# Linear attention and a snake-activated feed-forward layer on one core: the kv product in quarters of the tensor array

## The chip, the core and the metric

The kernel runs on one core of a Trainium2 chip. A core has five engines with queues of their own: TensorE (PE in the profile; its weight loads are listed apart as PEld), VectorE (DVE), ScalarE (ACT), GpSimd (POOL) and SyncE (SP). They wait for each other through semaphores. Matrix products read on-chip memory with 128 partitions and write to accumulators of eight banks per partition. The metric is the device time of one launch, in microseconds; the median of three runs of the kernel before is 287.68 us (287.46 to 288.37).

## The reference

The first half is a linear attention over 8 batches, 8 heads, 576 rows and 64 dimensions; the second a feed-forward layer with a snake activation over the 4608 rows.

```python
q_s = softmax(q, over the 64 dimensions)
k_s = softmax(k, over the 576 rows)
kv  = einsum('bhsd,bhse->bhde', k_s, v)          # 64 x 64 for each batch and head
x   = einsum('bhsd,bhde->bhse', q_s, kv)         # then heads side by side: 4608 x 512
h   = x @ w_in                                   # 4608 x 2048
g   = h + sin(alpha * h) ** 2 / alpha
out = g @ w_out                                  # 4608 x 512
```

## The kernel before

Rows. A batch has 576 rows, laid out as 64 partitions by J = 9 rows each. Eight heads are stored as four pairs `i` and two row halves `e`: partitions 0 to 63 hold heads of even number, partitions 64 to 127 those of odd number. So 128 partitions hold both, and a tile `st_q`, `st_k` or `st_v` is 128 x 4 x 9 x 64.

Attention of a batch. ACT takes the exponential of k into `ke` (bf16, line 118). v is cast into `vb`, where each head has 65 columns: 64 of v and one of ones, so that the product also gives the sum of the exponentials (lines 134 to 137, 299). `kv_mm(b, ii)` (line 163) handles two of the four `i`, that is two heads of each row half, in one go: for each of the nine j and each of the two row halves e, one product with 64 contracted rows, 128 weight columns (two heads of `ke`) and 130 moving columns (the same two heads of `vb`), summed over j in `kvp`, a tile of two accumulator banks, one for each e. Only the two diagonal blocks of 64 x 65 of each 128 x 130 result are used; the others mix two heads. `kv_norm` (line 176) takes the reciprocals of the sums (DVE, line 181), and two multiplies (line 184) put the diagonal blocks, divided by the sums, into `kbd`, a block-diagonal matrix whose other blocks were set to zero once. `attn_out` or `attn_chunk` (lines 220, 228) then multiplies `kbd` with the transposed, normalized exponentials of q (`qT`), two heads at a time, and copies the result to `xT`.

Feed-forward. For each of nine groups of 512 rows, `mm_h` (line 248) makes sixteen h blocks with four 512-column products each; ACT takes the sine, ACT, POOL or DVE the square; `combine` (line 264, DVE) writes `g`; `mm_o` (line 268) sums sixteen products into each of four outputs of the group, and `evac_o` copies and stores them.

Order. The order on each engine is the order in the program (a manual schedule). Batches 0 and 1 run at the start, where `kv_mm(b, 0)` and `kv_mm(b, 1)` are separate bursts of 18 products, each with its own `kvp` and `kv_norm` (lines 344 and 358, 451 and 454). The start of the feed-forward waits for batch 0. For batches 2 to 7 the two calls follow each other, 36 products in one burst, and one `kv_norm` (lines 516 to 518, and `attn_back`, lines 540 to 542). From batch 3 on the burst lies between the h and output products of the feed-forward groups, and its result is first used by `attn_out` several blocks later. PE gets a weight load (PEld) and a product from each call of `nc.tensor.matmul`, so a burst of 36 products is 72 instructions.

Of the kernel before, what the change touches and what calls it, by code (L numbers as in the profile page):

```python
# [15 lines left out]
F32 = mybir.dt.float32  # L16
BF16 = mybir.dt.bfloat16
AX = mybir.ActivationFunctionType
ALU = mybir.AluOpType
# [4 lines left out]
def kernel(  # L24
# [14 lines left out]
    nc = tc.nc  # L39
    ctx.enter_context(nc.allow_non_contiguous_dma(reason="layout"))  # L40
    B, H, S, D = q.shape
# [3 lines left out]
    J = 9  # L45
# [12 lines left out]
    small = ctx.enter_context(tc.tile_pool(name="small", bufs=2))  # L58
# [55 lines left out]
    A = {}  # L114
# [48 lines left out]
    def kv_mm(b, ii, pool, split=False):  # L163

        if ii == 0 or split:
            A["kvp", b] = pool.tile([128, 2, 512], F32, name="kvp", tag="a")
        kvp, ke, vt = A["kvp", b], A["ke", b], vb[b % 2]
        for j in range(J):
            for e in range(2):
                r = slice(64 * e, 64 * e + 64)  # L170
                nc.tensor.matmul(kvp[:, e, ii * 130:(ii + 1) * 130],  # L171
                                 ke[r, j, ii * 128:(ii + 1) * 128],
                                 vt[r, j, ii * 130:(ii + 1) * 130],
                                 start=(j == 0), stop=(j == J - 1))

    def kv_norm(b, i0=0, i1=2):

        kt, m = kbd[b % 2], i1 - i0
        kvr = small.tile([128, 2, 2, 2], F32, name="kvr")[:, :, 0:m]
        src = A["kvp", b][:, :, i0 * 130:i1 * 130].rearrange("p e (ii x c) -> p e ii x c", ii=m, x=2)  # L180
        nc.vector.reciprocal(kvr, src[:, :, :, :, D])
        for x in range(2):
            r = slice(64 * x, 64 * x + 64)
            nc.vector.tensor_tensor(kt[r, :, i0:i1, r], src[r, :, :, x, 0:D],  # L184
                                    kvr[r, :, :, x].unsqueeze(3).to_broadcast([64, 2, m, D]), op=ALU.mult)

    def q_tile(b):
        if ("qT", b) not in A:
# [153 lines left out]
    exp_half("k", 0, 1)  # L342
    warm_up(2)
    kv_mm(0, 0, ps_e, split=True)
    warm_up(3)
    kv_norm(0, 0, 1)
    tp1 = ps_e.tile([128, 8, 128], BF16, name="tp", tag="a")
    q_transpose_ii(0, 1, 0, 8, tp1)
# [7 lines left out]
    ACT_CP(A["qT", 0][:, 1, 0:8], tp1)  # L356
    ACT_CP(xT[:, 1, 0:MF], xp[1])
    kv_mm(0, 1, ps_e, split=True)
    kv_norm(0, 1, 2)
    xp = [ps_e.tile([128, 2, MF], F32, name="xp", tag="a")[:, 0] for _ in range(2)]  # L360
    for e in range(2):
# [35 lines left out]
    with ES:  # L397
# [51 lines left out]
        exp_to(A["qe", 1][:, 7:J], q78)  # L449
        take(os, 3)  # L450
        kv_mm(1, 0, ps_e, split=True)
        kv_norm(1, 0, 1)
        take(os, 3)
        kv_mm(1, 1, ps_e, split=True)
# [102 lines left out]
    for t in range(3, nT):  # L557
        b = t + 1 if t + 1 < B else None
# [60 lines left out]
```

## Time and profile before

| | |
|---|---|
| median of three runs | 287.68 us (287.46 to 288.37) |
| span of the profiled execution, first to last instruction | 285.8 us |
| median less span | 1.9 us |
| PE busy | 272.6 us, 95% |
| kv products, line 171 | 288, 9.9 us busy (union), 216 ns each |
| kv weight loads, line 171 | 288, 8.4 us busy, 93 ns each |
| h products, line 248 | 512 of them as `hp`, 129.0 us |
| output products, line 268 | 479 of them as `op`, 121.9 us |
| reciprocals, line 181 | 6 of 128x8 at 198 ns, 4 of 128x4 at 180 ns |
| multiplies into `kbd`, line 184 | 12 of 64x256 at 422 ns, 8 of 64x128 at 289 ns |

The page gives a span for the profiled execution and no other time of its own; its span is set beside the median of the runs. Busy time of a group is the union of its instructions, so overlapping ones count once; the mean is the recorded duration of one, which for a product includes its way through the pipeline (a 512-column product is recorded with 379 ns, while its successor starts 216 ns after it). "Idle before" is the time in which the engine did nothing before such an instruction. A few per cent of the product records are missing.

### The profile page before, as it was taken

How to read it: one execution, taken by the hardware profiler on the slowest of the kernel's cores; microseconds unless marked ns; L12 is line 12 of the kernel's file. 1: busy time of each engine (PE TensorE's matmuls, PEld its weight loads, DVE VectorE, ACT ScalarE, POOL GpSimd, SP SyncE). 2: the span in 40 equal slices, each digit the busy share in tenths (PEclk: the TensorE clock that was granted, in tenths of full speed). 3: DMA queues.
4: the chain of work that ended last, by engine and by line, in shares of the span. 5: the costliest groups of instructions: out<-in, count | busy, mean ns of one | idle time of the engine just before them, and what ended most of it. 6: DMA issues, size and time to landing. Idle time of an engine off the chain costs nothing.

```text
span 285.8 us, 4247 instructions
## 1 busy us (share of the span) xinstructions
PE 272.6 (95%) x1541; PEld 130.8 (46%) x1569; DVE 192.6 (67%) x291; ACT 226.0 (79%) x321; POOL 80.6 (28%) x75
## 2 busy tenths in 40 slices
PE   2899999999999999999999999999999999999994
PEld 1444454445454454444544454445444444444443
DVE  4857967999999658766785677667674555555321
ACT  4898748999489999899889988998877777777400
POOL 2869512773477480005300530041000000000000
PEclk9999999999999999999999999999999999999999
DMA  7999999843999984139711990016011111111242
GB/s 261 308 204 243 260 397 407 312 169 78 275 222 412 372 169 105 37 69 406 218 38 39 359 292 20 22 36 155 1 39 37 37 37 39 37 38 41 46 100 73
DMA packets 38581, 45.77 MB, mean 160 GB/s; under 512 B 16528, under 2 KB 22432, under 8 KB 38560
## 3 DMA queue, kind: packets, MB, share of 16 engines
q1 hardware_dynamic: 33376, 40.57, 46.3%
q0 software_dynamic: 4992, 4.79, 9.7%
q8 instruction: 12, 0.20, 0.3%
q10 hardware_dynamic: 192, 0.14, 0.2%
q14 instruction: 9, 0.07, 0.1%
HBM read 36.71 MB, written 9.44 MB: 161 GB/s over the span
## 4 chain that ended last, share of the span: by engine, by line
PE 74%; DVE 9%; DMA 7%; ACT 4%; issue 3%; POOL 2%; SPq 0%; ACTq 0%
PE op L268 33%; PE hp L248 33%; DMA st_v<-in_v_dram 5%; ACT s L254 3%; DVE g L264 2%; POOL s L258 2%; PE kvp L171 2%; DVE qs L150 2%; PE xp L220 2%; DMA st_q<-in_q_dram 1%; PE op L589 1%; PE hh L248 1%; DVE vb L137 1%; DVE qn L152 1%; DVE kbd L184 1%
## 5 line engine op out<-in xcount | busy, mean ns | idle before, releaser
L264 DVE SCALAR_TENSOR_TENSOR g<-s,inva_sb,hp 128x512 bf16<-128x512 f32 x130 | 96.0, 745 | 58.4 <-ACT s L256 54.2
L248 PE MATMUL hp<-xT,win 128*128 128x512 bf16 x512 | 129.0, 379 | 0.5
L268 PE MATMUL op<-wout,g 128*128 128x512 bf16 x479 | 121.9, 379 | 1.2 <-issue 0.6
L254 ACT ACTIVATE s<-hp,alpha_sb 128x512 f32<-128x512 f32 x130 | 87.8, 682 | 25.1 <-PE hp L248 22.6
L248 PEld LDWEIGHTS <-win 128*128 128x128 bf16 x576 | 56.3, 98 | 67.5 <-issue 0.8
L268 PEld LDWEIGHTS <-g 128*128 128x128 bf16 x560 | 54.1, 98 | 61.1 <-issue 0.4
L256 ACT ACTIVATE s<-s 128x512 f32<-128x512 f32 x111 | 69.9, 630 | 3.5
L152 POOL TENSOR_TENSOR qn<-qe,qs 128x1152 bf16<-128x1152 bf16 (+1 forms) x12 | 24.9, 2091 | 78.6 <-DVE qs L146 69.2
L258 POOL TENSOR_TENSOR s<-s 128x512 f32<-128x512 f32 x30 | 33.0, 1111 | 22.3 <-ACT s L254 22.0
L274 DVE COPY o<-op 128x512 f32<-128x512 f32 (+2 forms) x33 | 22.0, 668 | 9.7 <-PE op L268 5.8
L118 ACT ACTIVATE ke<-st_k 128x1152 bf16<-128x1152 f32 x16 | 17.9, 1151 | 5.0 <-DMA st_k<-in_k_dram 5.0
L118 ACT ACTIVATE qe<-st_q 128x1152 bf16<-128x1152 f32 (+3 forms) x18 | 17.7, 1025 | 2.1 <-DMA st_q<-in_q_dram 1.9
L145 DVE TENSOR_REDUCE qs<-qe 128x36 f32<-128x2304 bf16 x5 | 12.8, 2553 | 8.7 <-ACT qe L118 8.6
L268 PE MATMUL hp<-wout,g 128*128 128x512 bf16 x62 | 14.8, 379 | 0.2 <-issue 0.2
L223 DVE CAST xT<-xp 128x512 bf16<-128x512 f32 (+1 forms) x18 | 13.4, 742 | 0.0
L137 POOL CAST vb<-st_v 128x1152 bf16<-128x1152 f32 x10 | 11.3, 1163 | 6.5 <-DMA st_v<-in_v_dram 6.5
L171 PEld LDWEIGHTS <-ke 64*128 64x128 bf16 x288 | 8.4, 93 | 4.9 <-issue 1.9
L171 PE MATMUL kvp<-vb,ke 64*128 64x130 bf16 x288 | 9.9, 216 | 0.7 <-ACT vb L137 0.4
L118 ACT ACT_TABLE_LOAD x7 | 9.0, 1283 | 1.3 <-PEq L603 1.2
L248 PE MATMUL hh<-xT,win 128*128 128x512 bf16 x39 | 9.6, 379 | 0.1
L220 PE MATMUL xp<-qT,kbd 128*128 128x256 bf16 (+1 forms) x40 | 8.2, 286 | 0.4 <-DVE xT L223 0.3
L150 DVE TENSOR_REDUCE qs<-qe 128x16 f32<-128x1024 bf16 (+2 forms) x6 | 7.2, 1197 | 1.8 <-ACT qe L118 1.8
(79 smaller groups left out, 123.1 us busy)
## 6 DMA issues: line engine op xcount, KB each, us to landing
out_dram<-o SPq DMA_DIRECT2D x70, 128.0 KB, 2.3
st_q<-in_q_dram SPq DMA_DIRECT2D x6, 1152.0 KB, 6.7
st_k<-in_k_dram SPq DMA_DIRECT2D x6, 1152.0 KB, 8.9
st_v<-in_v_dram SPq DMA_DIRECT2D x6, 1152.0 KB, 10.2
st_k<-in_k_dram SPq DMA_DIRECT2D x4, 576.0 KB, 7.1
wout<-in_moe_w_out_dram POOLq DMA_DIRECT2D x4, 512.0 KB, 11.7
st_v<-in_v_dram SPq DMA_DIRECT2D x3, 576.0 KB, 9.4
win<-in_moe_w_in_dram POOLq DMA_DIRECT2D x6, 256.0 KB, 7.7
```

Of the source, the lines that this page charges most:

```text
L118: nc.scalar.activation(dst[:, :, ii * 128:(ii + 1) * 128].rearrange("p j (x d) -> p x j d", x=2), src[:, ii::2], AX.Exp)
L137: engs[ii](vv[:, 2 * ii:2 * ii + 2, :, 0:D], staged["v", b][:, ii::2])
L152: engs[ii % len(engs)].tensor_tensor(qn[:, ii, 0:j1].rearrange("p j (x d) -> p j x d", x=2), qe[:, ii], part.unsqueeze(3).to_broadcast([12 ...
L171: nc.tensor.matmul(kvp[:, e, ii * 130:(ii + 1) * 130], ke[r, j, ii * 128:(ii + 1) * 128], vt[r, j, ii * 130:(ii + 1) * 130], start=(j == 0 ...
L220: nc.tensor.matmul(xp[:, e, 0:n], kt[:, e, ii], qT[:, ii, j0:j1, e * 64:(e + 1) * 64], start=True, stop=True)
L248: nc.tensor.matmul(hp, win[:, ki, ni * 128:(ni + 1) * 128], xT[:, ki, t * MF:(t + 1) * MF], start=(ki == 0), stop=(ki == 3))
L254: nc.scalar.activation(s, hp, AX.Sin, scale=alpha_sb[:, ni:ni + 1])
L256: nc.scalar.activation(s, s, AX.Square)
L258: nc.gpsimd.tensor_tensor(s, s, s, op=ALU.mult)
L264: nc.vector.scalar_tensor_tensor(G[t][:, ni], in0=s, scalar=inva_sb[:, ni:ni + 1], in1=hp, op0=ALU.mult, op1=ALU.add)
L268: nc.tensor.matmul(acc, G[t][:, ni, j * 128:(j + 1) * 128], wout[:, ni, :], start=(ni == 0), stop=(ni == nN - 1))
L274: eng(o[:, cols], acc)
```

## The change

`kv_mm` makes two products for each one it made: for x = 0 and 1, one head h = 2 ii + x, with 64 weight columns of `ke`, 65 moving columns of `vb` and the result in partitions 64 x to 64 x + 63 of `kvp`. Contracted rows and output columns are both 64, so that each product uses one of four quarters of the array: row half e, column half x. The order is j, then e, then x. The result of a head pair takes 65 columns of `kvp` where it took 130, and only the diagonal blocks are computed. In `kv_norm` the reciprocal has half as many elements (the tile `kvr` loses its x axis, since the partitions now tell the heads apart), and the two multiplies read the same number of elements from the new places.

```diff
         for j in range(J):
             for e in range(2):
                 r = slice(64 * e, 64 * e + 64)
-                nc.tensor.matmul(kvp[:, e, ii * 130:(ii + 1) * 130],
-                                 ke[r, j, ii * 128:(ii + 1) * 128],
-                                 vt[r, j, ii * 130:(ii + 1) * 130],
-                                 start=(j == 0), stop=(j == J - 1))
+                for x in range(2):
+                    h = 2 * ii + x
+                    nc.tensor.matmul(kvp[64 * x:64 * x + 64, e, ii * 65:(ii + 1) * 65],
+                                     ke[r, j, h * 64:(h + 1) * 64],
+                                     vt[r, j, h * 65:(h + 1) * 65],
+                                     start=(j == 0), stop=(j == J - 1))
 
     def kv_norm(b, i0=0, i1=2):
 
         kt, m = kbd[b % 2], i1 - i0
-        kvr = small.tile([128, 2, 2, 2], F32, name="kvr")[:, :, 0:m]
-        src = A["kvp", b][:, :, i0 * 130:i1 * 130].rearrange("p e (ii x c) -> p e ii x c", ii=m, x=2)
-        nc.vector.reciprocal(kvr, src[:, :, :, :, D])
+        kvr = small.tile([128, 2, 2], F32, name="kvr")[:, :, 0:m]
+        src = A["kvp", b][:, :, i0 * 65:i1 * 65].rearrange("p e (ii c) -> p e ii c", ii=m)
+        nc.vector.reciprocal(kvr, src[:, :, :, D])
         for x in range(2):
             r = slice(64 * x, 64 * x + 64)
-            nc.vector.tensor_tensor(kt[r, :, i0:i1, r], src[r, :, :, x, 0:D],
-                                    kvr[r, :, :, x].unsqueeze(3).to_broadcast([64, 2, m, D]), op=ALU.mult)
+            nc.vector.tensor_tensor(kt[r, :, i0:i1, r], src[r, :, :, 0:D],
+                                    kvr[r].unsqueeze(3).to_broadcast([64, 2, m, D]), op=ALU.mult)
```

## The prediction

> **What bounds the kernel now.** I read the page first: busy line, slices, chain.
>
> ```profile
> PE 272.6 (95%) x1541; PEld 130.8 (46%) x1569; DVE 192.6 (67%) x291; ACT 226.0 (79%) x321; POOL 80.6 (28%) x75
> PE   2899999999999999999999999999999999999994
> PEclk9999999999999999999999999999999999999999
> PE 74%; DVE 9%; DMA 7%; ACT 4%; issue 3%; POOL 2%; SPq 0%; ACTq 0%
> ```
>
> TensorE (PE) is busy from the second slice on, at its full granted clock, and carries three quarters of the chain. Times of busy engines can hide pauses, so next the table of busy time by stretch, and the chain in order of time.
>
> ```profile
> 100.00:130.00 30.00, 29.84 (x171) 14.25 (x172) 21.14 (x31) 28.02 (x39) 6.42 (x4) 1.00 0.48 109
> 130.00:160.00 30.00, 29.68 (x170) 14.34 (x173) 20.64 (x29) 27.46 (x39) 6.48 (x4) 1.00 0.56 175
> ...
> 133.23 0.86 PE hp L248 x4
> 134.09 0.65 PE op L268 x3
> 134.74 0.86 PE hp L248 x4
> 135.61 1.13 PE kvp L171 x36
> ```
>
> The first number after the stretch's length is PE: 29.7 of 30 us. On the chain, four 512-column products take 0.86 us, 216 ns each, back to back, and the 36 kv products of a batch lie between them with nothing beside them: 1.13 us. From 15 us on, PE time is kernel time, almost one for one. So I need the price of the burst, from the view of its line and the timeline.
>
> ```profile
> L171 PEld LDWEIGHTS <-ke x288: 91/93/97, 9.5 to 196.1; 64*128 64x128 bf16 x144
> L171 PE MATMUL kvp<-vb,ke x288: 213/216/228, 9.8 to 196.2; 64*128 64x130 bf16 x144
> L171 PEldq EVENT_SEMAPHORE  x7: 51/51/51, 11.8 to 193.4; - x7
> ...
> 193.61 0.81 PE L268 MATMUL op<-wout,g 128*128 128x512 bf16 x3
> 194.26 1.03 PE L248 MATMUL hp<-xT,win 128*128 128x512 bf16 x4
> 195.22 1.19 PE L171 MATMUL kvp<-vb,ke 64*128 64x130 bf16 x36
> ...
> 195.21 1.02 PEld L171 LDWEIGHTS <-ke 64*128 64x128 bf16 x36 [0.42 <-ACT s L256]
> 195.21 0.11 PEld L171 LDWEIGHTS <-ke 64*128 64x128 bf16 x4 [0.42 <-ACT s L256]
> ```
>
> The last product is recorded with 216 ns, most of it pipeline, so 36 starts spread over 1.19 - 0.22 = 0.97 us: 18 steps (9 rows j, two head pairs), each with two products, one per row half. A step takes 0.97/17 = 57 ns. The stream rate is 216/512 = 0.42 ns a column; 130 columns are 55 ns, and 2 ns are left. So the two row halves already run side by side, each limited by its stream, and all weight loads (93 ns from start to end) hide behind it. The last row is the same load in a 30 ns window: four weight loads have started by its end, so instructions that are already in PE's queue start within some 5 ns of each other.
>
> **The change, part by part.**
> *Removed:* per step, two products of 130 columns on 128 output columns: 57 ns x 18 = 1.03 us a batch, 8.2 us in all eight, all but the first 0.5 us on the path.
> *Added:* per step, four products of 65 columns and four loads of 64 columns, in four quarters. Stream alone: 65 x 0.42 + 2 = 30 ns if all four quarters run side by side: 18 x 27 = 0.49 us less per batch. That is the best case, 8 x 0.49 = 3.9 us. No row of before shows column halves side by side, nor a 64-column load.
> *Hand-over of instructions:* a step now holds eight instructions instead of four. PE's sequencer must supply them, 144 per batch instead of 72. How fast it can is not shown directly, so I bound it. The semaphore instruction that stands just before the last burst in program order ran at 193.4 us, the burst began at 195.21: between them the timeline has 7 products and 6 loads. The same 13 stand between the two in the bursts at 135.5 and 165.4. I read that as a queue with room for about 14 instructions, which the sequencer keeps full. Then 72 - 14 = 58 instructions were handed over within the 1.02 us of a burst: at most 17.6 ns each. The lower bound is that it never limits: 8 instructions in 30 ns, under 4 ns each, as in the queue's own starts. Between the two I take 11 ns, by the only rows that time the sequencer itself: in the trace's start times that semaphore instruction runs 8 to 16 ns (five cases, mean 11) after the product that freed a place. With 11 ns, a batch of 144 takes (144 - 14) x 11 = 1.43 us against 1.03: +0.40 us, six times (batches 2 to 7), +2.4 us. Batches 0 and 1 have their 72 in two bursts each: (72 - 14) x 11 = 0.64 against 0.51: +0.12, four times, +0.5 us. Sum +2.9 us. Ends: at 17.6 ns, 2.29 - 1.03 = 1.26, six times, and 1.02 - 0.51, four times: +9.6 us; at under 4 ns, -3.9 us.
> The Trainium skill, "TensorEngine Tiling (Array Packing)", section Instruction Overhead, speaks against the change: each product has some 60 cycles of overhead, and a dimension that is already small should not pay for a tiling factor. By the rule, taken as a cost per instruction at the 2.4 GHz that "TensorE: Matmul & The Clock Gate" gives, four products would need 100 ns a step, two 50 (under the 57 seen); 43 x 18 x 8 = +6.2 us as an estimate. The trace speaks against a cost at the start of each product, since starts lie some 5 ns apart, and not against one at the hand-over.
> *Weight loads:* the nearest rows are two loads on an idle PE near 3 us, when 512-column products still lay 427 ns apart: a bf16 load of 128 columns took 104 ns, an f32 one 176. If the 72 ns are what a slow way of loading costs and go by columns, 64 columns cost 36 ns more there, 18 at twice the pace; hidden behind a 30 ns stream if quarters load independently: nothing. At the other end, if a weight column takes as long as a moving one and the two quarters of a row half load and multiply strictly in turn, a step is 4 x 27 = 108 ns: 51 x 18 x 8 = +7.3 us. Below nothing isn't possible, since loads cost nothing now. I take nothing: today's loads hide fully in a stream.
> The page named above says, under Restrictions, that column tiling excludes fast weight load; no row of before shows such a load.
> *Switch of tile shape:* the pauses around a burst stay two per burst, 0.3 us of load idle time together; same before and after, 0.
> *DVE:* in kv_norm the reciprocal of 128x8 (198 ns) becomes 128x4 (180 ns, the row of the split batches): 18 ns x 6, off the path since DVE is busy 21 of 30 us there. The multiplies (422 and 289 ns) keep shape and count. kv_norm waits for the burst's last product; behind it on DVE stand the g combines, and those feed PE; in batch 5 the burst ended at 166.6 and the reciprocal started at 167.73, so 0.4 us of delay is covered. In batches 0 and 1 no cover exists (PE waits for kbd at 13.98): that is in the sum.
> *Queues:* no DMA is added or moved on SP, ACT or POOL; no wait is added. 576 more PE instructions are to be fetched; the instruction queue now takes 0.3% of the DMA engines, so 0.
>
> **Sum.** Span 285.8 + 2.9 = 288.7; the median 287.7 lies 1.9 above the span, so 290.6 us.
>
> **The rivals.**
> *Four quarters at once (faster).* Place: the bursts. It decides when the hand-over is under 1.03 / 130 = 7.9 ns an instruction and loads of column halves do not hinder each other. For it: today's row halves overlap perfectly, loads hide, starts 5 ns apart. Against: needs all three at once on 27 ns streams. Full price -3.9 us: 283.8.
> *Loads stay behind products (no difference).* Before, the trace shows a load pulled ahead of one waiting product and never of more (more was never needed). If one is the limit, a product starts no sooner than a load's time after the last but one: 2 x 30 = 60 ns a step, +3 x 144 = +0.4 us: 288.1. The same comes of column halves that run in turn, 2 x 28 = 56 ns: the change then does nothing of what it says.
> *Quarters fully in turn (slower by more).* 108 ns a step, +7.3: 295.0. Against it: loads of the next step run under the present stream today.
> *A new wait* for kv_norm: 1.1 us of slack in batch 5, so only above 17 ns an instruction.
>
> **How the numbers follow.** Measurement tells 0.3%, 0.86 us, from no change. Hand-over limit of about 9 to 16 ns: 0.36 (own range 288.6 to 294.6). Fully in turn or worse: 0.13. No difference, by loads or a hand-over near 8 ns: 0.14. Faster: 0.37. The range reaches from the full gain, 283.8, to 294.6, the upper part of the hand-over case; beyond it lie some 0.12. Faster 0.37, same 0.14, slower 0.49.
>
> **What would show it.** In the profile after: the kv line with 576 products and 576 loads; the burst's 72 products in about 1.6 us on PE instead of 1.19, with starts evenly spread (an empty queue) after the first 14 or so instructions, for the hand-over. Starts in groups of four every 30 ns, 0.7 us in all, would show the first rival; groups of two every 30 ns the second; single products some 27 ns apart, each behind its load, the third. My forecast fails first if the 11 ns is wrong: the sequencer's pace was only inferred from five start times.

## The result, and the profile after

The changed kernel takes 286.07 us (285.69 to 286.57, 4 runs) against 287.84 us for the kernel before (four runs): a ratio of 0.994 (95% interval 0.992 to 0.996), 1.8 us faster. A second, longer comparison (first experiment) gives 0.9945 (0.9925 to 0.9964). The forecast was 290.6 us, a slower kernel; the direction was wrong.

The page of the kernel after, its busy line, chain shares and the kv groups (line 173 is the product in `kv_mm`, line 183 the reciprocal):

```profile
PE 270.0 (95%) x1828; PEld 128.3 (45%) x1857; DVE 191.8 (67%) x291; ACT 225.9 (79%) x321; POOL 80.6 (28%) x75
PE 81%; DMA 7%; DVE 6%; POOL 2%; issue 2%; ACT 1%; SPq 0%; ACTq 0%
...
L173 PE MATMUL kvp<-vb,ke 64*64 64x65 bf16 x576 | 6.9, 194 | 0.0
L173 PEld LDWEIGHTS <-ke 64*64 64x64 bf16 x576 | 5.7, 106 | 4.4 <-ACT s L258 1.3 <-ACT vb L318 0.8 <-issue 0.6
L183 DVE RECIPROCAL kvr<-kvp 128x4 f32<-128x4 f32 x6 | 1.0, 172 | 0.0
```

PE has 288 products and 288 loads more, and is busy 2.6 us less; the kv products' union fell from 9.9 to 6.9 us, with twice as many. A load of 64 columns takes longer than one of 128 did (106 ns, 93 before), and DVE's reciprocal shrank by 26 ns. The price of one burst, from the table of busy time by stretch for the kv line alone, before and then after (behind the stretch's length stand the busy times of PE and PEld with their instructions; the bursts of batches 4 and 5 before, 4 to 6 after):

```profile
105.60:106.90 1.30, 1.20 (x36) 1.02 (x36) 1.00 2.04 202
135.50:136.80 1.30, 1.19 (x36) 1.02 (x36) 1.00 1.03 407
```

```profile
106.10:107.10 1.00, 0.80 (x72) 0.69 (x72) 1.00 0.82 179
135.60:136.60 1.00, 0.80 (x72) 0.69 (x72) 1.00 1.03 406
165.00:166.00 1.00, 0.78 (x72) 0.67 (x72) 1.00 1.04 412
```

72 products in quarters take 0.80 us where 36 in halves took 1.20: 0.40 us less per burst, against 0.49 for the ideal of 30 ns a step and +0.40 in the forecast. On the chain in order of time the whole of it shows, 1.13 us before, in the bursts of batches 5 and 6 now:

```profile
134.82 0.86 PE hp L250 x4
135.68 0.73 PE kvp L173 x72
...
164.27 0.86 PE hp L250 x4
165.13 0.71 PE kvp L173 x72
```

How the burst runs inside can be read from the trace's start times. These are the products of batch 6, ns from the first, one step of four to a column, one quarter to a row:

```
0    53   88   118  150  179  215  244  277  306  342  371  401  437  466  498  528  563
3    55   92   121  153  183  218  248  280  309  345  374  405  441  470  504  533  569
7    59   95   124  157  186  222  251  283  313  348  378  408  444  475  511  542  578
10   62   98   128  160  189  225  254  287  316  352  386  417  453  483  519  550  586
```

For eleven steps the four quarters start within 10 ns of each other, after the first step one every 32 ns: all four run at once. Then the groups open up, until at the end products start some 8 ns apart on average and the weight loads follow each other every 8 or 9 ns: a product and its load every 8.4 ns, 4.2 ns an instruction. That is the look that the forecast named for an empty queue; only the sequencer fills it two and a half times as fast as the forecast took.

But eight batches with 0.40 us each would be 3.2 us, and 1.8 came out. The experiments are about both halves of this: what sets the pace of a burst, and where the rest of the gain went.

### The profile page after: what moved, and what is told of

Same layout as the page of the kernel before. It is cut to its first block, busy times and chain, and to the rows that moved or that the text cites. A ratio compares the mean times of both kernels' runs of the same rounds, so it can differ in the third digit from the quotient of the medians.

```text
span 284.6 us, 4822 instructions
## 1 busy us (share of the span) xinstructions
PE 270.0 (95%) x1828; PEld 128.3 (45%) x1857; DVE 191.8 (67%) x291; ACT 225.9 (79%) x321; POOL 80.6 (28%) x75
## 4 chain that ended last, share of the span: by engine, by line
PE 81%; DMA 7%; DVE 6%; POOL 2%; issue 2%; ACT 1%; SPq 0%; ACTq 0%
PE hp L250 35%; PE op L270 34%; PE hp L270 5%; DMA win<-in_moe_w_in_dram 3%; PE hh L250 2%; DMA st_v<-in_v_dram 2%; DVE g L266 2%; DMA st_k<-in_k_dram 2%; PE xp L222 2%; PE kvp L173 1%; PE op L591 1%; DVE vb L137 1%; POOL win L108 1%; DVE qs L150 1%; ACT s L256 1%
## 5 line engine op out<-in xcount | busy, mean ns | idle before, releaser
L118 ACT ACTIVATE qe<-st_q 128x1152 bf16<-128x1152 f32 (+3 forms) x18 | 17.6, 1024 | 2.2 <-DMA st_q<-in_q_dram 2.0
L137 POOL CAST vb<-st_v 128x1152 bf16<-128x1152 f32 x10 | 11.3, 1164 | 6.5 <-DMA st_v<-in_v_dram 6.5
L266 DVE SCALAR_TENSOR_TENSOR g<-s,inva_sb,hh 128x512 bf16<-128x512 f32 x10 | 7.1, 742 | 1.6 <-POOL s L260 1.6
L173 PEld LDWEIGHTS <-ke 64*64 64x64 bf16 x576 | 5.7, 106 | 4.4 <-ACT s L258 1.3
```

What stands on the lines that cost most here:

```text
L118: nc.scalar.activation(dst[:, :, ii * 128:(ii + 1) * 128].rearrange("p j (x d) -> p x j d", x=2), src[:, ii::2], AX.Exp)
L137: engs[ii](vv[:, 2 * ii:2 * ii + 2, :, 0:D], staged["v", b][:, ii::2])
L266: nc.vector.scalar_tensor_tensor(G[t][:, ni], in0=s, scalar=inva_sb[:, ni:ni + 1], in1=hp, op0=ALU.mult, op1=ALU.add)
```

## The experiments

Where a diff below shows a list `QUARTERS`, `kv_mm` and `kv_norm` hold both forms, and the list names the batches that get quarters. The kernel before ran beside each set of experiments on the same chip, and the ratios are to it.

### Which batches pay

The changed kernel again:

> The changed kernel again, for a tight ratio beside the two halves of it. Theory (only the bursts of batches 4 to 7 lie where PE alone sets the end): 4 x 0.42 us = -1.7 us, 286.0. Rival (every burst counts for its full 0.42 us, and the first runs were unlucky by a late weight transfer at 17.7 us): -3.0 to -3.4 us, 284.5.

Measured: 285.92 us beside 287.72 of the kernel before, ratio 0.9945 (0.9925 to 0.9964).

```diff
+QUARTERS = (4, 5, 6, 7)
...
+                if b in QUARTERS:
+                    for x in range(2):
...
```

> Quarters only in the kv products of batches 4 to 7, halves as before in 0 to 3. Theory: the same gain as the whole change, -1.7 us (ratio 0.994). Rival (every burst counts): half of the whole change's gain, whatever that is; with -1.7 for the whole, -0.9.

Measured: 286.18 us, ratio 0.9942 (0.9930 to 0.9954).

```diff
+QUARTERS = (0, 1, 2, 3)
```

> Quarters only in the kv products of batches 0 to 3. Theory: the 1.6 us of PE time that they save are taken back by v's transfer at 41 us and by VectorE and the v transfer between 64 and 82 us: 0, at most -0.4 us. Rival (every burst counts): the same as the late half, -0.9 to -1.7 us.

Measured: 287.42 us, ratio 0.9996 (0.9978 to 1.0014), medians 0.3 us apart.

So four bursts of the eight batches carry the gain: the late half alone is as fast as the whole, within the intervals, and the early half alone can't be told from the kernel before. 4 x 0.40 = 1.6 us is about the measured gain (1.7 us by the late half's ratio). The rival that counts every burst falls.

### Where the early gain goes

The same weight load (the same place in PE's order, bursts left out) can be found in two traces. Its start, less its start before, shows where a kernel gains and loses. In us, positive is later than before; the columns are the early half, batches 1 to 3 alone (a run told below), the whole change (the trace of its second measurement) and the late half:

```
                              before at   early   1 to 3   whole   late
after batch 1                    44.3     -0.50   +1.01   -0.42   +0.24
ahead of batch 2's burst         66.9     -0.50   +1.02   -0.40   +0.24
after it                         68.5     -0.90   +0.63   -0.79   +0.24
after the products with q of 2   73.6     -0.57   +0.95   -0.61   +0.24
ahead of batch 3's burst         81.2     -0.58   +0.94   -0.61   +0.24
after it                         82.8     -0.97   +0.55   -1.01   +0.24
first products with kv of 3      89.4     -0.52   +1.00   -0.42   +0.25
ahead of batch 4's burst        103.2     -0.51   +0.99   -0.41   +0.26
after batch 5's burst           136.7     -0.51   +0.99   -1.20   -0.53
after batch 7's burst           196.3     -0.41   +0.99   -2.04   -1.28
```

The first row differs by what happened at the start of each execution, which scatters (below). From there the three kernels with quarters in batches 2 and 3 tell the same: each burst gains 0.39 to 0.40 us; of batch 2's, 0.2 to 0.3 is lost by 73.6 us; by 89.4 all that both had gained is gone; the four late bursts keep theirs. The waits of PE between 66 and 95 us say on what (us in total, number, the longest). Before, and then the kernel with quarters in batches 0 to 3:

```profile
PE xp L220 <- DVE xT L223: 0.3, 1, 0.3
PE op L268 <- issue: 0.2, 1, 0.2
```

```profile
PE xp L235 <- DVE xT L238: 0.8, 2, 0.6
PE hp L243 <- DMA qT<-qn: 0.2, 1, 0.2
PE op L283 <- issue: 0.2, 1, 0.2
```

PE gets earlier to the products with batch 2's transposed q, and waits 0.2 us for the transposing transfer; and it waits 0.5 us more at 88 to 92 us, where the attention result of batch 3 has one accumulator tile that DVE must empty, in its order, between the g blocks. In that stretch PE is busy all the same, as the page says, but its pace is that of the others. The chain of the kernel before, in order of time, had them there:

```profile
65.12 1.27 DVE qs L150
...
71.84 6.25 DMA st_v<-in_v_dram
78.11 3.25 DVE vb L137 x2
81.36 2.67 DVE g L264 x4
85.08 2.73 DVE g L264 x4
87.85 1.29 ACT s L254 x2
...
90.44 1.05 POOL s L258
...
94.05 1.03 PE op L268 x4
```

The late half, without quarters there, has the old line: 0.3 us, once.

Two attempts to release this stretch. First, v's transfer for batch 3 earlier:

```diff
     exp_q(2)
     exp_k(2)
+    load("v", v, 3)
     os = o_stream(1)
...
     q_transpose_dma(2, halves=True)
-    load("v", v, 3)
```

> The changed kernel with the transfer of v for batch 3 issued some 6 us earlier, behind the exponentials of batch 2; its cast stays on VectorE. Theory that VectorE's work between 64 and 92 us takes the early gain: the transfer's wait of 0.3 us goes, no more: -0.0 to -0.3 us against the changed kernel. Rival (the transfer takes it): -0.8 to -1.2 us, 284.9.

Measured: 287.04 us beside 288.35 of the kernel before on this chip, ratio 0.9961 (0.9947 to 0.9974): no gain over the change; by the two ratios rather 0.5 us less, with overlapping intervals. Then with the cast on ScalarE:

```diff
-    cast_v(3, [DVE_CP, DVE_CP])
+    cast_v(3, [ACT_CP, ACT_CP])
```

> The same, and the cast of v for batch 3 (3.1 us on VectorE at 78 us) moves to ScalarE, which stands idle for 3 us at 74.5. VectorE theory: VectorE is free 3 us earlier and the gain of the early bursts passes on: -0.5 to -1.2 us against the changed kernel, 285.0. Rival (ScalarE, 92% busy from 80 to 100 us, is then late with its sines): 0 or slower.

Measured: 286.99 us, ratio 0.9963 (0.9946 to 0.9980). The gain expected from VectorE did not come. PE's waits in the same stretch, of this last kernel, show why:

```profile
PE hp L230 <- DMA qT<-qn: 0.9, 2, 0.7
PE xp L222 <- DVE xT L225: 0.3, 1, 0.3
```

The wait at 88 us is back at 0.3, but the transfer of v now runs ahead of the transposes of q, and PE waits 0.9 us for those instead; the kernel with the transfer alone has the same two waits. The stall moved to the next input that was late. Whether the transfer of v or VectorE's cast had held PE, these two kernels cannot tell, since the new wait covers either.

Half of the cast on ScalarE, transfer untouched:

```diff
-    cast_v(3, [DVE_CP, DVE_CP])
+    cast_v(3, [DVE_CP, ACT_CP])
```

> The changed kernel with the second half of the cast of v for batch 3 on ScalarE (1.2 us) instead of VectorE (1.6 us), the transfer where it was. ScalarE waits 1.4 us at 80 us for an accumulator that VectorE frees behind this cast. If that wait holds the early gain: -0.4 to -0.8 us against the changed kernel. If the sines and squares on ScalarE pace the stretch from 78 to 94 us: 0, or slower by up to 0.5 us.

Measured: 286.79 us beside 287.73, ratio 0.9967 (0.9952 to 0.9983): no gain, as expected if ScalarE paces the stretch; its interval overlaps that of the change, so the loss isn't sure. Its trace fits: VectorE, done with its half of the cast, stands idle for 1.29 us before the first g at 81.89 us, which needs ScalarE's sine and GpSimd's square of it.

### Does added time cost there?

A copy of the burst, with 16 moving columns, ahead of the real one in batches 4 to 7:

```diff
             if n == 0:
+                if b >= 4:
+                    kv_mm(b, 0, ps_a, n=16)
+                    kv_mm(b, 1, ps_a, n=16)
                 kv_mm(b, 0, ps_a)
```

> In batches 4 to 7 the burst of the changed kernel is preceded by a copy of itself with 64 weight columns and only 16 moving columns, 72 products more, with no switch of tile shape between; the result is unchanged. Supply theory (4.2 ns an instruction once the queue of some 14 is empty): the whole of the second half runs at 33.5 ns a step with loads evenly 8.4 ns apart, and the 288 instructions take 274 x 4.2 = 1.15 us. Rival (streams of 65 columns set the second half): groups of four every 30 to 31 ns, 18 x 27 + 18 x 30.5 = 1.03 us. By either, PE sets the end there, so +2.0 to +2.3 us against the changed kernel, 288.1. Rival for the path: PE has slack, less than +1 us.

Measured: 288.89 us, ratio 1.0028 (1.0013 to 1.0042), that is 0.8% or 2.4 us above the change's 0.9945. On its chain the burst (144 products, of which the first ten start beside the last h product and are not counted here) has

```profile
166.53 1.29 PE kvp L173 x134
```

against 0.71 us: 0.58 us more, four times 2.3 us. PE sets the end there one for one. The last of the 144 starts 1164 ns after the first, 1.16 us for 288 instructions, near the 1.15 that 4.2 ns for all but 14 make. But this total doesn't tell the theories apart: the copy's steps, with streams of a quarter of the length, take 31.6 ns too, not the 27 of the rival, and with them the rival's sum rises from 1.03 to 1.12 us, close to it as well. The spacing does: from about the 26th of the 36 steps on (expected from the 19th), loads follow each other every 8 or 9 ns, some 33 ns a step, not in groups of four every 30 to 31. In the last five steps a load starts 7 to 13 ns after the product before it in its quarter, against at most 2 ns in the copy, and its own product starts 21 to 26 ns after it. So neither the stream nor an earlier load holds it: the instruction itself comes late, as the supply theory says. Which part of the way to the engine sets the 4.2 ns isn't shown. And before the queue is empty, it isn't the 65-column stream that sets the step.

The same copies in batches 2 and 3 alone:

> The changed kernel with the 72 products of 16 columns put before the bursts of batches 2 and 3 alone, 0.58 us of TensorE time each, 1.16 us in all; the result is unchanged. Theory (there PE has slack that the quarters widened, some 0.4 us a burst): +0.0 to +0.5 us against the changed kernel, ratio to the kernel before 0.994 to 0.996. Rival (PE sets the pace there as in batches 4 to 7): +1.2 us, ratio 0.9985.

Measured: 287.74 us beside 287.73, ratio 0.9989 (0.9972 to 1.0005). The rival's number, against the theory of plain slack. In its trace, the wait at 88 us is 0.3 us as before, as slack would have it, but

```profile
PE hp L230 <- DMA qT<-qn: 1.0, 1, 1.0
```

appears, and on the chain before that wait stands

```profile
71.05 4.39 DMA qT<-qn
```

The second transposing transfer of batch 2's q was issued at 71.05 us, as in the first trace of the change (70.99), but took 4.39 us to land instead of 2.86. Of its 16 semaphore updates 15 came by 73.91 us and the last at 75.44. Its last two 4-byte packets moved at 74.39 us, just as a 16 KB packet of the instruction queue ended (73.35 to 74.40 us); no other trace of this case has such a packet between 72 and 76 us. So the transfer's end stood, by all appearance, behind a fetch of instructions, not behind a later PE; that the added products brought the fetch there is likely and not shown. Against that trace of the change, whose start differs by less than 0.1 us, this one is 1.6 us later by 103 us, and 0.9 us of it arises at this one wait. So time taken from PE in batches 2 and 3 is worth next to nothing; what time added there costs by itself, without the late transfer, this run cannot tell, and the theory of slack is neither shown nor refuted.

### Is it the start?

All profiles with quarters in batch 0 that I had by then started the feed-forward layer later than the two with halves, as the last pieces of v and w_in landed later (18.0 to 19.6 us against 17.8 for the same weight load). If the quarters caused it, batch 0 had better keep its halves.

```diff
+QUARTERS = (1, 2, 3, 4, 5, 6, 7)
```

> Quarters in batches 1 to 7, halves in batch 0. In all profiles with quarters in batch 0, the v and weight transfers of the first 18 us landed later than in the two with halves there. Start theory (the quarters in batch 0 delay the start by 0.3 to 1.7 us and so cost what batches 1 to 3 gain): -2.2 to -2.9 us against the kernel before, ratio 0.990 to 0.992, faster than the change. Rival (those landings scatter from run to run, whatever batch 0 does): as the whole change, -1.6 to -1.8, ratio 0.994.

Measured: 286.62 us beside 288.26, ratio 0.9938 (0.9919 to 0.9956): as the whole change; the start theory's 0.990 to 0.992 only touches the interval's end.

```diff
+QUARTERS = (0,)
```

> Quarters in batch 0 alone. Start theory: slower than the kernel before by 0.5 to 1.2 us, ratio 1.002 to 1.004. Rival (scatter): the same, at most 0.2 us faster.

Measured: 288.79 us, ratio 1.0012 (0.9993 to 1.0032): not to be told from no change; the upper part of the interval reaches the start theory's numbers.

```diff
+QUARTERS = (1, 2, 3)
```

> Quarters in batches 1, 2 and 3 alone. Start theory: -0.8 to -1.2 us, ratio 0.996 to 0.997. Rival (what these batches gain is taken back between 82 and 89 us, where PE waits for attention results that VectorE, ScalarE and GpSimd make): 0 to -0.5 us, ratio 0.998 to 1.000, as for batches 0 to 3.

Measured: 288.04 us, ratio 0.9989 (0.9975 to 1.0002). The rival's range.

The profiles settle what the times leave open: with halves in batch 0, two of these kernels' traces have that weight load at 18.6 and 19.6 us. The landings scatter with halves in batch 0 too. The start theory falls at the size that it named; a smaller effect of batch 0 is not excluded.

### What limits a step

```diff
                 for x in range(2):
                     h = 2 * ii + x
-                    nc.tensor.matmul(kvp[64 * x:64 * x + 64, e, ii * 65:(ii + 1) * 65],
+                    w, n = (64, 65) if j in (0, J - 1) else (32, 16)
+                    nc.tensor.matmul(kvp[64 * x:64 * x + w, e, ii * 65:ii * 65 + n],
...
```

> For j = 1 to 7 each product has only 32 weight columns and 16 moving columns; three quarters of the kv sums are left out. Streams and loads shrink to a third or less, the number of instructions stays. Theory (from some 60 instructions into a burst the sequencer's supply is the limit, 4.2 ns an instruction): weight loads still follow each other every 8.4 ns, a step still takes 33 ns. Rival (a 64-column load or a 65-column stream is the limit): a step shrinks to 15 to 20 ns.

This kernel leaves out sums and ran once (287.0 us), so only its trace is used. The table by stretch for this line, 0.21 us inside the first run of small products (PE, PEld):

```profile
165.16:165.37 0.21, 0.21 (x32) 0.21 (x28) 1.00 1.00 395
```

The products of the seven steps, 28 in all, start at 165.164, .202, .227, .252, .277, .302 and .327 us: after the first, 25 ns a step, neither theory's number. The test did not tell them apart as meant: the switch between shapes of 64 and 32 columns pauses the loads (0.14 us from the last product of the larger shape to the next load, 0.10 us on the way back), long enough at 4.2 ns an instruction to refill a queue of 14, so the supply never became the limit. What it does show: four products with their loads can pass in 25 ns, 3.1 ns an instruction, when the queue is full; with 64-column loads and the same 16 moving columns the copies above had 31.6. In both, a quarter's next load starts 2 ns after its product, and the product some 23 ns (32 weight columns) or 30 ns (64) after its load, which makes the 25 and the 31.6. So the weight load sets the step before the queue is empty, and the supply after it. The 25 ns are a time of one quarter, not of an instruction, since four quarters start within 10 ns; whether a shorter load would go below 25 was not run.

## Why the prediction was wrong

*What bounds the kernel.* "From 15 us on, PE time is kernel time, almost one for one" holds from 103 us to the end (removing 0.40 us four times gave 1.7, adding 0.58 four times took 2.4) and fails before: the slices showed PE at nine tenths or more from 15 us on, and I read full as decisive, while the chain in order of time had DVE, ACT, POOL and a DMA between 64 and 92 us (shown above). The removed time of the bursts in batches 2 and 3 was priced in full and was worth nothing that could be measured (ratio 0.9996 with quarters in batches 0 to 3 alone).

*Hand-over of instructions.* This step failed and turned the sign. The upper bound of 17.6 ns stands, and the queue of some 14 instructions agrees with the bursts, though it is a reading (13 instructions lie between semaphore and burst four times, 17 before batch 2's); the 11 ns do not stand: 4.2 ns is measured. With it the step's own formula gives (144 - 14) x 4.2 = 0.55 us for a burst, and first to last start were 0.59. So with 4.2 ns this step alone would have led to the first rival's gain; that only half of it came lies in the step above. The start times of the semaphore instruction, 8 to 16 ns after a product (four of the seven, by the trace), were taken for one interval of the sequencer; at 4.2 ns they are two to four. The value lay near the lower end, which the row "four loads begun within 30 ns" had pointed to. The prediction's range for 9 to 16 ns, 288.6 to 294.6, ends by its own formula at 15 ns; 16 gives 295.7.

*Weight loads.* Taken as nothing, and nearly right: a 64-column load lasts 106 ns instead of 93 and four quarters load independently, but the step is 32 ns and not 30 before the queue empties, since the loads are its limit.

*The rule of 60 cycles.* The Trainium skill, "TensorEngine Tiling (Array Packing)", section Instruction Overhead, gave an estimate of +6.2 us if read as a cost of each instruction. Measured: four products in 25 ns with short operands, 32 with those of the change, so read per instruction it does not hold here. Read per tile of the array it does not conflict with the 25 ns.

*DVE, queues, switch of shape.* Right: DVE's reciprocal shrank from 198 to 172 ns off the path, no queue was touched, and the pauses around a burst stayed (0.42 us of load idle ahead of it, 0.16 us of PE idle behind it in both). The instructions to be fetched, put at nothing, cost no wait that the change's profile shows.

*The rivals.* "Four quarters at once" was the right mechanism, its conditions all met (4.2 is under 7.9 ns), its place in the bursts right; its price of 3.9 us was 8 x 0.49, and 4 x 0.40 is what counts. Loads that stay behind products and quarters in turn did not occur: by the trace, loads are pulled ahead of up to three waiting products. The new wait came, though not at kv_norm: 0.2 us for transposed q and 0.5 us for the accumulator at 88 us, both in batches 2 and 3.

Still open: what the added copies in batches 2 and 3 would cost without the late transposing transfer; and what batches 0 and 1 are worth, which the scatter of the start covers.

## What to carry to other kernels

A product that computes blocks nobody reads can be cut into quarters of the array, and they do run side by side, down to streams of 65 columns; price such a step by the longest of the stream, the load and its instructions at the sequencer's pace (eight here), and take that pace from a burst long enough to empty the queue. A full engine isn't yet the engine that sets the end: before a gain is multiplied by the number of places, look at each place on the chain in order of time. When a price is known only between two bounds of opposite sign, say so by the range and don't settle it by an indirect row.

## What the runs showed of the hardware

- Late in long bursts of short products an instruction reaches PE about every 4.2 ns (8 to 9 ns for a load and its product), in bursts of 144 and of 288 instructions. That this is the sequencer's pace once a queue of some 14 instructions is empty is the reading that fits both.
- Four products in quarters, each with its own load, start within 10 ns of each other and pass in 25 ns with 32 weight and 16 moving columns, in 31.6 with 64 and 16, and in 32 with 64 and 65.
- A change of tile shape between 64 x 64 and 64 x 32 pauses the loads: 96 ns from the last small product's start to the next load in this trace, 143 ns the other way.
- In one trace the last of 16 updates of a transposing transfer came 1.5 us after the 15th, with a 16 KB packet of the instruction queue ahead of its last packets; PE waited 1.0 us.
- The same early weight load came between 17.8 and 19.6 us in different executions, with halves as with quarters in batch 0; in several of these traces PE waited there for the landing of w_in (0.6 to 1.1 us) or a cast of v (0.2 to 1.3 us).
